# Retention attention and a snake MLP on one core: keys and values of three batches taken in runs of 64 tokens, half of the in-chunk scores left out

## The chip, the cores and the metric

The kernel runs on one core of one Trainium2 chip. The metric is the device time of one execution, in microseconds. The time before is 309.64 us, the median of three runs that lie between 309.6 and 310.09 us.

## The reference

Eight batches of 576 tokens pass through a retention layer with eight heads of 64 elements, and the result, as 4608 rows of 512, through a two-layer MLP with a snake activation:

```
scores = scale * q @ k.T                      # per batch and head
Dmat   = gamma_h ** (i - j) where i >= j, else 0
attn   = (scores * Dmat) @ v
x      = attn, heads side by side             # 4608 x 512
h      = x @ w_in                             # 512 -> 2048
g      = h + sin(alpha * h)**2 / (alpha + 1e-9)
out    = g @ w_out                            # 2048 -> 512
```

Because `Dmat` is zero above the diagonal, a key meets only queries that are not earlier than itself.

## The kernel before

The decay `gamma ** (i - j)` is split into a factor on the keys and one on the queries, both applied when the float32 input is cast to float16 (`cast`, with the factors in the constant tile `cn`). The tokens of a batch are taken as two parts of 256 (`p` = 0, 1) and a tail of 64 (`p` = 2). A part holds two chunks of 128 tokens. Inside a chunk the layer is computed directly: scores, mask, values. What earlier chunks contribute arrives through a 64x64 state for each head and chunk (`outer`, `more`, `to_state`, `add_states`).

**Layout.** `load` brings a part into a tile of 128 partitions by 8 heads by 2 x 64 floats. Partitions 0 to 63 hold the first chunk and 64 to 127 the second. Partition `i` of a chunk holds tokens `2i` and `2i + 1`, which lie next to each other in memory, so a packet of the transfer carries 512 bytes. The index `r` (0 or 1) names the token of the pair. `crossed` turns the cast q and k by DMA transposes into `qT` and `kT`. The tails of two batches share one tile (`raws`, one tile for a pair of batches, each for q, k and v); they come in packets of 256 bytes.

**In-chunk attention.** `scores` is made of matmuls of 64x64 weights. For each head group (`y`, `z`), each half `r` of the keys, each chunk `g` and each half `t` of the heads there is one with 128 query columns: 16 for one call, 64 for a batch. `masked` multiplies a bank pair by a mask of 256 columns (both `r`, 128 queries each) on VectorE and writes float16. `values` multiplies the masked scores by v, again with 64x64 weights and 128 query columns, 64 matmuls for a batch. It comes in two rounds: first those whose rows differ from the bank's half (`same` false), then the others. Between them stands a mark on GpSimd (`told`): a no-op in GpSimd's queue waits for the first round, and the first matmul of the second round waits for that no-op.

**MLP.** Tokens go through the MLP in blocks of 512: the eight batches without their tails, and then the eight tails together. For a block `project(n, u)` makes 128 hidden units (four matmuls of 512 columns), `sine` and `square` run on ScalarE (some squares on VectorE or GpSimd), `product` on VectorE, and `gemm2` makes the output 128 rows at a time. `finish` copies a 128-row result to `osb` and stores it in two transfers.

**Order.** All engines take their instructions in the order in which the program writes them. Up to block 2 that order is written by hand, line by line. From block 3 on a loop writes it: the loop's pass `n` has 16 units `u`; unit `u` issues `project(n, u)`, `sine(n, u)`, what `at_unit(u, ...)` has put there, the square, the product, a quarter of `gemm2(n - 1, ...)`, and then what `behind(u, ...)` has put there. Pass `n` also carries the attention of batch `n + 1` (scores in units 3 and 8, values and state products in unit 12) and, for batch `n + 2`, the casts on GpSimd (units 3 to 8, in the order k0 v0 k1 v1 q0 q1, where the digit is `p`), the states (unit 12) and the transposes (units 13 and 15). The first three loads of batch `n + 3` stand behind units 13 to 15, the other three in units 0 to 2 of the next pass; for batch 5 all six stand in units 0 to 5 of pass 3. The tails of batches `2j` and `2j + 1` are loaded in units 7 to 9 of pass `j + 3`, cast by GpSimd in units 12 to 14 and transposed in unit 15.

All of these loads, transposes and stores are issued by SyncE's queue (SP), one after the other. Each of them waits, besides its data, for the transfer issued eight places earlier on this queue.

```
for i, (nm, p) in enumerate(("k0", "v0", "k1", "v1", "q0", "q1")):
    if n == 3:
        at_unit(i, lambda nm=nm, p=p: load(5, nm, int(p)))
    elif n < 6 and i > 2:
        at_unit(i - 3, lambda nm=nm, p=p: load(n + 2, nm, int(p)))
    if n < 5 and i < 3:
        behind(13 + i, lambda nm=nm, p=p: load(n + 3, nm, int(p)))
    if n < 6:
        at_unit(3 + i, lambda nm=nm, p=p: cast(n + 2, nm, int(p), G_))
```

Of the kernel before, what the change touches and what calls it, by code (L numbers as in the profile page):

```python
# [17 lines left out]
def kernel(  # L18
# [11 lines left out]

    nc = tc.nc

    B, H, S, D = q.shape
# [4 lines left out]
    FC = FF // P  # L40
    KT = DM // P
    NBLK = NT // 512

    gamma = 1.0 - 2.0 ** (-5.0 - np.arange(H, dtype=np.float64))
    scale = 1.0 / np.sqrt(D)
    hi, ii = np.divmod(np.arange(P), 64)
    cn_np = np.zeros((P, 52), dtype=np.float64)
    for h in range(H):
        for r in range(2):
            cn_np[:, 2 * h + r] = gamma[h] ** (64 - (2 * ii + r))  # L50
            cn_np[:, 16 + 2 * h + r] = scale * gamma[h] ** (2 * ii + r - 64)
        cn_np[:, 32 + h] = gamma[h] ** (64 - ii)
        cn_np[:, 40 + h] = scale * gamma[h] ** (ii - 64)
    for a in range(4):
# [8 lines left out]

    ident = const.tile([P, P], F16, tag="ident", bufs=1)
    mask = const.tile([P, 5 * 64], F16, tag="mask", bufs=1)
    cn = const.tile([P, 52], F32, tag="cn", bufs=1)
    fac = {"k": cn[:, 0:16], "q": cn[:, 16:32]}
# [24 lines left out]
    def halves(n):  # L92
        return slice(64 * n, 64 * n + 64)
# [9 lines left out]
    T = {}  # L103

    def load(b, nm, p):
        if p < 2:
            t_ = work.tile([P, H, 2 * D], F32, tag="raw", bufs=6, name=nm + "32")
            nc.sync.dma_start(  # L108
                t_, src[nm][b, :, 256 * p : 256 * p + 256, :].rearrange("h (i r) d -> i h (r d)", r=2)
            )  # L110
        else:
            if b % 2 == 0:
                raw[b, nm, 2] = work.tile([P, H, D], F32, tag="raws", bufs=3, name=nm + "s32")
            t_ = raw[b - b % 2, nm, 2]
            nc.sync.dma_start(t_[halves(b % 2)], src[nm][b, :, 512:576, :].rearrange("h i d -> i h d"))
        raw[b, nm, p] = t_
# [3 lines left out]
    def cast(b, nm, p, eng, ys=(0, 1)):  # L120
# [15 lines left out]
        if p == 2:  # L136
            if nm == "v":
                copy(eng, dst.rearrange("p h d -> p (h d)"), t_.rearrange("p h d -> p (h d)"))
            else:
                eng.tensor_tensor(  # L140
                    dst.rearrange("p a t d -> p t a d"),
                    t_.rearrange("p (t a) d -> p t a d", t=2),
                    fac_s[nm].rearrange("p (t a) -> p t a", t=2).unsqueeze(3).to_broadcast([P, 2, 4, D]),
                    MULT,
                )
        elif nm == "v":
            h0, h1 = 4 * ys[0], 4 * ys[-1] + 4
            copy(
                eng,
                dst[:, h0:h1].rearrange("p h r d -> p (h r d)"),  # L150
                t_[:, h0:h1].rearrange("p h x -> p (h x)"),
            )
        else:
            a0, a1 = 2 * ys[0], 2 * ys[-1] + 2
            n = 2 * (a1 - a0)
            eng.tensor_tensor(  # L156
                dst[:, a0:a1].rearrange("p a r t d -> p t (a r) d"),
                t_.rearrange("p (t a) x -> p t a x", t=2)[:, :, a0:a1].rearrange("p t a (r d) -> p t (a r) d", r=2),
                fac[nm]
                .rearrange("p (t x) -> p t x", t=2)[:, :, 2 * a0 : 2 * a1]  # L160
                .unsqueeze(3)
                .to_broadcast([P, 2, n, D]),
                MULT,
            )
# [63 lines left out]
    class Attention:  # L228
        def __init__(self, b):
            self.b = b  # L230
            self.both = {}
# [87 lines left out]
        def scores(self, p, y, tag):  # L319
            kT, qT = T[self.b, "k", p], T[self.b, "q", p]  # L320
            sc = psum.tile([P, 2, 512], F32, tag=tag, bufs=1, name="sc")
            for z in range(2):
                a = 2 * y + z
                for r in range(2):
                    for g in range(2):
                        for t in range(2):
                            c = 256 * z + 128 * r
                            matmul(  # L328
                                sc[halves(g), t, c : c + 128],
                                kT[halves(t), 2 * a + r, halves(g)],  # L330
                                qT[halves(t), 2 * a : 2 * a + 2, halves(g)],
                                start=(z == 0 and r == 0), stop=True, skip_group_check=True,
                            )
            self.sc[p, y] = sc

        def masked(self, p, y):
            sc = self.sc.pop((p, y))
            ret = work.tile([P, 2, 512], F16, tag="ret", bufs=4, name="ret")
            nc.vector.tensor_tensor(  # L339
                ret.rearrange("p t (z x) -> p (t z) x", z=2),  # L340
                sc.rearrange("p t (z x) -> p (t z) x", z=2),
                mask[:, 0:256].unsqueeze(1).to_broadcast([P, 4, 256]),
                MULT,
            )
            self.ret[p, y] = ret

        def values(self, p, same, *tags, relay=None):
# [12 lines left out]
            made = []  # L360
            for x in range(2):
                for r in range(2):
                    for e in range(2):
                        for g in range(2):
                            t = g if same else 1 - g
                            c = 256 * x + 128 * g
                            m = 256 * e + 128 * r
                            made.append(matmul(  # L368
                                o[t][halves(e), c : c + 128],
                                v16[halves(g), 4 * t + 2 * x + e, r, :],  # L370
                                self.ret[p, x][halves(g), t, m : m + 128],
                                start=(not same and x == 0 and r == 0), stop=False, skip_group_check=True,
                            ))
            if not same and relay is not None:
# [201 lines left out]
    def make_constants():  # L576
# [8 lines left out]
        for g in range(2):  # L585
# [6 lines left out]
            nc.gpsimd.affine_select(  # L592
                out=m, in_=m, compare_op=ge, fill=0.0, base=0, pattern=[[1, 64]], channel_multiplier=-1,
            )

    with tc.manual_schedule():
        nc.scalar.dma_start(cn, cn_dram.ap())
# [479 lines left out]
        at[4].to_state(3, G_)  # L1077
        at[4].to_state(2, G_)
        crossed(4, 0, "q")

        h, m = cycle(("h2", "h0", "h1")), cycle(("m0", "m1"))
        ON_A = (4, 5, 6, 8, 9)
        for n in range(3, NBLK):
# [54 lines left out]
            for u in range(16):  # L1138
# [63 lines left out]
```

## Time and profile before

| | |
|---|---|
| median of the runs | 309.64 us |
| the profiled execution's own time | 310.26 us |
| its span, first to last instruction | 308.5 us |
| granted TensorE clock, mean | 0.989 |
| TensorE busy | 295.6 us, 96% |
| VectorE busy | 206.7 us, 67% |
| ScalarE busy | 181.0 us, 59% |
| GpSimd busy | 135.2 us, 44% |
| moved by DMA | 49.83 MB in 102676 packets |
| packets under 512 bytes | 44640 |

The busy time is the time in which at least one instruction of the engine was under way. In the views of instructions in order of time, a row gives start and length in microseconds, engine, line of the kernel, operation, output and inputs, shape and count; a bracket at its end gives the idle time of the engine before it and what ended that. `PE` is TensorE, `DVE` VectorE, `ACT` ScalarE, `POOL` GpSimd, `SPq` the issuing of transfers on SyncE. Pass 3 of the loop fills about 109 to 140 us of the span, pass 4 140 to 171, pass 5 171 to 202 and pass 6 202 to 233. In what follows a pass is called block 3, 4, 5 or 6.

### The profile page before, as it was taken

What the parts mean: (1) busy time and instruction counts of PE and PEld (TensorE: products, weight loads), DVE (VectorE), ACT (ScalarE), POOL (GpSimd) and SP (SyncE); (2) the same over time, 40 slices, a digit from 0 to 9 for tenths busy, and PEclk for the clock granted to TensorE, in tenths of its full rate; (3) what the DMA queues carried; (4) which work ended last, traced back from release to release, by engine and by line L of the source; (5) the groups of instructions that cost most, each with busy time, mean ns of one, the idle gap of its engine ahead of it and who ended that gap; (6) DMA issues with size and microseconds to landing.
All of it is one profiled execution on the core that took longest, in us unless ns stands there. A gap on an engine that the chain in (4) does not pass through costs nothing.

```text
span 308.5 us, 7866 instructions
## 1 busy us (share of the span) xinstructions
PE 295.6 (96%) x3257; PEld 151.0 (49%) x3257; DVE 206.7 (67%) x298; ACT 181.0 (59%) x286; POOL 135.2 (44%) x150
## 2 busy tenths in 40 slices
PE   6679899999999999999999999999999999999995
PEld 5555456555444544454445444544454454444443
DVE  1686899899669798657765776666666746555600
ACT  1348864675444857674768476857674456555411
POOL 4684772288759589469266926650030000000000
PEclk9599999999999999999999999999999999999999
DMA  7999999999998899879898999763431111111232
GB/s 206 292 228 216 225 249 266 218 262 276 204 213 233 125 231 260 171 111 218 219 261 123 235 213 259 116 130 75 102 70 36 34 36 36 35 34 37 46 89 69
DMA packets 102676, 49.83 MB, mean 162 GB/s; under 512 B 44640, under 2 KB 98160, under 8 KB 102640
## 3 DMA queue, kind: packets, MB, share of 16 engines
q1 hardware_dynamic: 98048, 44.97, 67.0%
q0 software_dynamic: 4224, 4.19, 8.0%
q8 instruction: 25, 0.41, 0.6%
q10 hardware_dynamic: 368, 0.17, 0.2%
q14 instruction: 11, 0.09, 0.1%
HBM read 36.74 MB, written 9.44 MB: 150 GB/s over the span
## 4 chain that ended last, share of the span: by engine, by line
PE 75%; DMA 12%; POOL 5%; issue 3%; ACT 2%; SPq 1%; DVE 0%; POOLq 0%; DVEq 0%; ACTq 0%
PE ops L546 36%; PE hps L503 32%; DMA v<-in_v_dram 5%; DMA q<-in_q_dram 4%; DMA qT<-q 3%; PE o L368 2%; PE sc L328 2%; POOL k L156 1%; POOL q L156 1%; PE kv L269 1%; SPq L108 1%; ACT s_t L511 1%; POOL kvs L311 1%; POOL s L303 1%; PE o L390 1%
## 5 line engine op out<-in xcount | busy, mean ns | idle before, releaser
L546 PE MATMUL ops<-w_out,gT 128*128 128x512 f16 (+2 forms) x592 | 142.5, 374 | 0.3 <-ACT kvs L97 0.2
L527 DVE SCALAR_TENSOR_TENSOR gT<-ss_t,inva,hps 128x512 f16<-128x512 f16 x144 | 106.3, 746 | 52.8 <-ACT ss_t L520 46.0
L511 ACT ACTIVATE s_t<-hps,alpha_t 128x512 f16<-128x512 f32 x144 | 97.4, 687 | 70.7 <-PE hps L503 69.1
L503 PE MATMUL hps<-xT,w_in 128*128 128x512 f16 (+1 forms) x544 | 126.6, 367 | 0.4 <-DMA w_in<-in_moe_w_in_dram 0.2
L503 PEld LDWEIGHTS <-w_in 128*128 128x128 f16 x608 | 58.6, 98 | 64.6 <-DMA w_in<-in_moe_w_in_dram 0.7
L546 PEld LDWEIGHTS <-gT 128*128 128x128 f16 x592 | 56.2, 98 | 64.5 <-issue 0.8
L522 DVE TENSOR_TENSOR ss_t<-s_t 128x512 f16<-128x512 f16 x72 | 40.5, 564 | 17.9 <-ACT s_t L511 17.5
L339 DVE TENSOR_TENSOR ret<-sc,mask 128x1024 f16<-128x1024 f32 x32 | 38.4, 1219 | 3.1 <-PE sc L328 3.1
L520 ACT ACTIVATE ss_t<-s_t 128x512 f16<-128x512 f16 x62 | 38.8, 631 | 0.9
L156 POOL TENSOR_TENSOR q<-q,cn 128x1024 f16<-128x1024 f32 (+1 forms) x16 | 27.4, 1722 | 13.7 <-DMA q<-in_q_dram 13.6
L97 ACT COPY osb<-ops 128x512 f32<-128x512 f32 (+1 forms) x34 | 19.7, 582 | 21.9 <-PE ops L546 20.3
L156 POOL TENSOR_TENSOR k<-k,cn 128x1024 f16<-128x1024 f32 (+1 forms) x13 | 21.7, 1671 | 20.8 <-DMA k<-in_k_dram 16.1
L140 POOL TENSOR_TENSOR ks<-ks,cn 128x512 f16<-128x512 f32 x4 | 4.2, 1044 | 34.2 <-PE o L368 34.2
L311 POOL TENSOR_TENSOR kvs<-s,kvs 128x256 f32<-128x256 f32 x22 | 16.4, 747 | 2.6 <-ACT kvs L97 0.9
L97 ACT CAST xT<-o 128x1024 f16<-128x1024 f32 (+1 forms) x14 | 13.2, 957 | 6.1 <-PE o L390 6.1
L503 PE MATMUL hps<-xS,w_in 128*128 128x512 f16 x64 | 16.4, 379 | 0.0
L522 POOL TENSOR_TENSOR ss_t<-s_t 128x512 f16<-128x512 f16 x10 | 10.8, 1086 | 11.4 <-ACT s_t L511 11.4
L310 POOL TENSOR_TENSOR s<-kvs,cn 128x256 f32<-128x256 f32 x22 | 13.6, 620 | 0.6 <-ACT kvs L97 0.4
L99 POOL CAST v<-v 128x1024 f16<-128x1024 f32 (+1 forms) x10 | 10.2, 1030 | 8.3 <-DMA v<-in_v_dram 8.3
L303 POOL TENSOR_TENSOR s<-kvs,cn 128x256 f16<-128x256 f32 x19 | 12.7, 674 | 1.1 <-issue 0.4
L368 PE MATMUL o<-ret,v 64*64 64x128 f16 x512 | 11.5, 219 | 0.8 <-DVE ret L339 0.4
L328 PE MATMUL sc<-qT,kT 64*64 64x128 f16 x512 | 11.5, 225 | 0.6 <-DMA qT<-q 0.4
(58 smaller groups left out, 139.2 us busy)
## 6 DMA issues: line engine op xcount, KB each, us to landing
out_dram<-osb SPq DMA_DIRECT2D x70, 128.0 KB, 2.5
k<-in_k_dram SPq DMA_DIRECT2D x16, 512.0 KB, 6.8
q<-in_q_dram SPq DMA_DIRECT2D x16, 512.0 KB, 6.9
v<-in_v_dram SPq DMA_DIRECT2D x16, 512.0 KB, 6.3
w_in<-in_moe_w_in_dram POOLq DMA_DIRECT2D x4, 512.0 KB, 12.5
w_out<-in_moe_w_out_dram POOLq DMA_DIRECT2D x4, 512.0 KB, 11.4
ks<-in_k_dram SPq DMA_DIRECT2D x8, 128.0 KB, 4.5
qs<-in_q_dram SPq DMA_DIRECT2D x8, 128.0 KB, 3.6
```

Source lines behind the costliest of these rows:

```text
L97: eng.copy(d_, s_)
L156: eng.tensor_tensor(dst[:, a0:a1].rearrange("p a r t d -> p t (a r) d"), t_.rearrange("p (t a) x -> p t a x", t=2)[:, :, a0:a1].rearrange( ...
L311: nc.gpsimd.tensor_tensor(self.kvs[:, c], s32, self.kvs[:, c], ADD)
L328: matmul(sc[halves(g), t, c : c + 128], kT[halves(t), 2 * a + r, halves(g)], qT[halves(t), 2 * a : 2 * a + 2, halves(g)], start=(z == 0 an ...
L339: nc.vector.tensor_tensor(ret.rearrange("p t (z x) -> p (t z) x", z=2), sc.rearrange("p t (z x) -> p (t z) x", z=2), mask[:, 0:256].unsque ...
L368: made.append(matmul(o[t][halves(e), c : c + 128], v16[halves(g), 4 * t + 2 * x + e, r, :], self.ret[p, x][halves(g), t, m : m + 128], sta ...
L503: matmul(hps_of[n, fc][0][:, cols], w_in16[:, a, fc * P : (fc + 1) * P], xs[n][:, a, cols], start=(a == 0 and part != 1), stop=(a == KT - ...
L511: nc.scalar.activation(s_t, hps, mybir.ActivationFunctionType.Sin, bias=0.0, scale=alpha_t[:, fc : fc + 1],)
L520: nc.scalar.activation(ss_t, s_t, mybir.ActivationFunctionType.Square)
L522: eng.tensor_tensor(ss_t, s_t, s_t, MULT)
L527: nc.vector.scalar_tensor_tensor(gT[n][:, fc, :], ss_t, inva[:, fc : fc + 1], hps, MULT, ADD)
L546: matmul(ops[n, c, cols.start][:, cols], gT[n][:, fk, c * P : (c + 1) * P], w_out16[:, fk, cols], start=(fk == 0), stop=(fk == FC - 1), sk ...
```

## The change

For batches 5, 6 and 7 (`HALVED = 5`) k and v of a part are laid out otherwise: partition `i` of a chunk holds tokens `i` and `64 + i` of it, so `r` = 0 is the first half of the chunk's keys and `r` = 1 the second. The queries keep their layout. A key of the second half meets only queries of the second half, and those are the columns `i >= 32` of both query halves. So the matmuls for `r` = 1 in `scores` and `values` take 64 columns (two runs of 32) where they took 128, and the mask multiply 192 where it took 256, with a mask of its own (`mask_halved`, made on GpSimd in unit 1 of block 3). The decay factors of the keys get 16 further columns in `cn`.

A load of k or v in this layout is made of four transfers of 64 partitions with packets of 256 bytes, where it was one of 128 partitions with packets of 512 bytes.

Three things are moved. The first three loads of batch 5 stand before the loop, the other three in units 0 to 2 of block 3. The tails of `j` = 1 go from block 4 to block 5, and those of `j` = 2 from block 5 to units 0 to 8 of block 6; `j` = 0 and `j` = 3 stay. In blocks 4 to 6 the square of unit 6 goes from ScalarE to VectorE, and that of unit 10 from VectorE to ScalarE.

```diff
+    HALVED = 5
-    cn_np = np.zeros((P, 52), dtype=np.float64)
+    cn_np = np.zeros((P, 68), dtype=np.float64)
+            cn_np[:, 52 + 2 * h + r] = gamma[h] ** (64 - (64 * r + ii))
...
     def load(b, nm, p):
-        if p < 2:
+        if p < 2 and b >= HALVED and nm != "q":
+            t_ = work.tile([P, H, 2 * D], F32, tag="raw", bufs=6, name=nm + "32")
+            for g in range(2):
+                for r in range(2):
+                    s0 = 256 * p + 128 * g + 64 * r
+                    nc.sync.dma_start(
+                        t_[halves(g), :, r * D : r * D + D], src[nm][b, :, s0 : s0 + 64, :].rearrange("h i d -> i h d")
+                    )
+        elif p < 2:
...
# scores
                 for r in range(2):
+                    i0, n = (32, 64) if self.halved and r else (0, 128)
...
-                                sc[halves(g), t, c : c + 128],
+                                sc[halves(g), t, c : c + n],
-                                qT[halves(t), 2 * a : 2 * a + 2, halves(g)],
+                                qT[halves(t), 2 * a : 2 * a + 2, 64 * g + i0 : 64 * g + 64],
...
# masked
+            n, seen = (192, mask_halved) if self.halved else (256, mask[:, 0:256])
-                mask[:, 0:256].unsqueeze(1).to_broadcast([P, 4, 256]),
+                seen.unsqueeze(1).to_broadcast([P, 4, n]),
...
# values
-                                o[t][halves(e), c : c + 128],
+                                o[t][halves(e), c : c + 128].rearrange("p (r i) -> p r i", r=2)[:, :, i0:64],
-                                self.ret[p, x][halves(g), t, m : m + 128],
+                                self.ret[p, x][halves(g), t, m : m + n],
...
+    def make_mask_halved():
+
+        nc.gpsimd.memset(mask_halved, 1.0)
+        for g in range(2):
+            for c0, n in ((0, 64), (128, 32)):
+                m = mask_halved[halves(g), c0 : c0 + 2 * n].rearrange("p (r i) -> p r i", r=2)
+                nc.gpsimd.affine_select(
+                    out=m, in_=m, compare_op=mybir.AluOpType.is_ge, fill=0.0,
+                    base=0, pattern=[[1, 2], [2, n]], channel_multiplier=-1,
+                )
...
# before the loop, and in it
         crossed(4, 0, "q")
+        load(5, "k", 0)
+        load(5, "v", 0)
+        load(5, "k", 1)
...
-                if n == 3:
-                    at_unit(i, lambda nm=nm, p=p: load(5, nm, int(p)))
-                elif n < 6 and i > 2:
+                if n < 6 and i > 2:
...
-            for j in range(n - 3, min(n - 2, 4)):
+            for j, u0 in {3: ((0, 7),), 5: ((1, 7),), 6: ((2, 0), (3, 7))}.get(n, ()):
                 for i, nm in enumerate("kqv"):
-                    at_unit(7 + i, lambda j=j, nm=nm: load(2 * j, nm, 2), lambda j=j, nm=nm: load(2 * j + 1, nm, 2))
-                    at_unit(12 + i, lambda j=j, nm=nm: cast(2 * j, nm, 2, G_))
-                at_unit(15, lambda j=j: crossed(2 * j, 2))
+                    at_unit(u0 + i, lambda j=j, nm=nm: load(2 * j, nm, 2), lambda j=j, nm=nm: load(2 * j + 1, nm, 2))
+                    at_unit(u0 + 5 + i, lambda j=j, nm=nm: cast(2 * j, nm, 2, G_))
+                at_unit(u0 + 8, lambda j=j: crossed(2 * j, 2))
+            if n == 3:
+                at_unit(1, make_mask_halved)
...
-                    square(n, u, A_ if A and u in ON_A else V)
+                    square(n, u, A_ if A and u in (ON_A if n < 4 else (4, 5, 8, 9, 10)) else V)
```

More of the change, by code (lines that the diff above doesn't have):

```diff
@@ L65 @@
     mask = const.tile([P, 5 * 64], F16, tag="mask", bufs=1)
-    cn = const.tile([P, 52], F32, tag="cn", bufs=1)
-    fac = {"k": cn[:, 0:16], "q": cn[:, 16:32]}
+    mask_halved = const.tile([P, 3 * 64], F16, tag="mask_halved", bufs=1)
+    cn = const.tile([P, 68], F32, tag="cn", bufs=1)
+    fac = {"k": cn[:, 0:16], "q": cn[:, 16:32], "halved k": cn[:, 52:68]}
     fac_s = {"k": cn[:, 32:40], "q": cn[:, 40:48]}
@@ L158, in cast @@
                 t_.rearrange("p (t a) x -> p t a x", t=2)[:, :, a0:a1].rearrange("p t a (r d) -> p t (a r) d", r=2),
-                fac[nm]
+                fac["halved k" if nm == "k" and b >= HALVED else nm]
                 .rearrange("p (t x) -> p t x", t=2)[:, :, 2 * a0 : 2 * a1]
@@ L230, in __init__ @@
             self.b = b
+            self.halved = b >= HALVED
             self.both = {}
@@ L338, in masked @@
             ret = work.tile([P, 2, 512], F16, tag="ret", bufs=4, name="ret")
+            n, seen = (192, mask_halved) if self.halved else (256, mask[:, 0:256])
             nc.vector.tensor_tensor(
-                ret.rearrange("p t (z x) -> p (t z) x", z=2),
-                sc.rearrange("p t (z x) -> p (t z) x", z=2),
-                mask[:, 0:256].unsqueeze(1).to_broadcast([P, 4, 256]),
+                ret.rearrange("p t (z x) -> p (t z) x", z=2)[:, :, 0:n],
+                sc.rearrange("p t (z x) -> p (t z) x", z=2)[:, :, 0:n],
+                seen.unsqueeze(1).to_broadcast([P, 4, n]),
                 MULT,
@@ L362, in values @@
                 for r in range(2):
+                    i0, n = (32, 64) if self.halved and r else (0, 128)
                     for e in range(2):
```

## The prediction

> **What bounds the kernel.** I read the page's head first, then the busy time by stage, with borders at unit 12 of each block.
>
> ```profile
> PE 295.6 (96%) x3257; PEld 151.0 (49%) x3257; DVE 206.7 (67%) x298; ACT 181.0 (59%) x286; POOL 135.2 (44%) x150
> ```
> ```profile
> 104.00:134.20 30.20, 30.20 (x348) 14.72 (x340) 24.38 (x34) 20.81 (x33) 19.62 (x19) 1.00 0.90 196
> 134.20:165.25 31.05, 31.05 (x351) 15.13 (x344) 21.23 (x28) 20.96 (x34) 18.98 (x19) 1.00 0.97 204
> 165.25:196.30 31.05, 31.05 (x351) 15.09 (x344) 21.27 (x28) 20.97 (x34) 19.00 (x20) 1.00 0.94 204
> 196.30:227.70 31.40, 31.40 (x291) 14.92 (x285) 20.37 (x29) 21.50 (x34) 9.65 (x15) 1.00 0.54 104
> ```
>
> The columns are the stretch, its length, busy PE, PEld, DVE, ACT and POOL (with counts), granted clock, DMA share and GB/s. From 104 us on PE is busy all the time at full clock; DVE and ACT are busy two thirds of it, POOL less. So a TensorE microsecond saved here is a microsecond of the kernel, and one lost by waiting is lost. DMA is nearly always occupied in the second and third stretch: that is where a dearer transfer can hurt. The change touches nothing of weight before 104 us (the constant tile grows from 52 to 68 columns).
>
> **The narrower matmuls.** PE in unit 12 of block 4, and the tails' scores, in order of time:
>
> ```profile
> 162.34 1.03 PE L503 MATMUL hps<-xT,w_in 128*128 128x512 f16 x4
> 163.29 0.64 PE L368 MATMUL o<-ret,v 64*64 64x128 f16 x32
> 163.76 0.72 PE L269 MATMUL kv<-v,k 64*64 64x64 f16 x64
> 164.30 0.41 PE L368 MATMUL o<-ret,v 64*64 64x128 f16 x16
> ...
> 235.57 0.71 PE L425 MATMUL scs<-qTs,kTs 64*64 64x64 f16 x64
> 236.22 1.04 PE L546 MATMUL ops<-w_out,gT 128*128 128x512 f16 x4
> ```
>
> Lengths overlap, so I take start to start. 32 matmuls of 128 columns take 163.76 - 163.29 = 0.47 us, 14.7 ns each; 64 of 64 columns take 164.30 - 163.76 = 0.54 us, 8.4 ns each. A narrowed one saves 6.3 ns. Half of the 64 score and 64 value matmuls of a batch are narrowed: 64 per batch, 192 in all, 1.2 us, all on the path (0.2 us each for scores and values of a batch). Bounds: 0 if wide and narrow ones in turns all run at the wide pace, or if reading and writing two runs of 32 columns costs what it saves; 1.4 us if half the time goes (7.3 ns). I take 1.2, because the 64-column row is the same 64x64 form, and the tails' scores (64 in 0.65 us with the return to wide matmuls) agree with it.
>
> **The mask and the squares.** Neither is on the path.
>
> ```profile
> L339 DVE TENSOR_TENSOR ret<-sc,mask 128x1024 f16<-128x1024 f32 x32 | 38.4, 1219 | 3.1 <-PE sc L328 3.1
> L520 ACT ACTIVATE ss_t<-s_t 128x512 f16<-128x512 f16 x62 | 38.8, 631 | 0.9
> L587 POOL TENSOR_SCALAR_AFFINE_SELECT mask<-mask 64x256 f16<-64x256 f16 x2 | 0.8, 420 | 0.1
> 161.67 0.69 ACT L511 ACTIVATE s_t<-hps,alpha_t 128x512 f16<-128x512 f32 x1 [1.04 <-PE hps L503]
> ```
>
> A mask multiply falls from 1024 to 768 columns, at most from 1.22 to 0.91 us, twelve times: some 3 us of DVE that nobody waits for. The square of 0.63 us that comes to ACT in unit 10 fits into the 1.04 us that ACT is idle before the next sine; the one that leaves ACT in unit 6 goes to a DVE with 10 us idle in each block. If that cover were gone, a square would cost its 0.63 us in three blocks. The new mask is five small POOL operations, each at most 0.42 us, so at most 2.1 us before the first cast of block 3. The last two casts there waited for their loads (rows below), and POOL has 4.5 us before PE needs its mark.
>
> **The loads.** This is where it can go wrong. SP in order of time: two rows of block 3, the border of blocks 3 and 4, two pairs of tails later.
>
> ```profile
> 109.88 0.57 SPq L108 DMA_DIRECT2D k<-in_k_dram  x1
> ...
> 118.79 1.77 SPq L108 DMA_DIRECT2D q<-in_q_dram  x2
> ...
> 137.10 0.57 SPq L108 DMA_DIRECT2D k<-in_k_dram  x1
> 137.73 0.80 SPq L108 DMA_DIRECT2D v<-in_v_dram  x1
> 138.57 3.63 SPq L179 DMA_TRANSPOSE kT<-k  x1
> 142.32 1.49 SPq L179 DMA_TRANSPOSE qT<-q  x1
> 143.91 1.21 SPq L179 DMA_TRANSPOSE kTs<-ks  x1
> 145.21 1.38 SPq L179 DMA_TRANSPOSE qTs<-qs  x1
> 146.68 1.18 SPq L539 DMA_DIRECT2D out_dram<-osb  x2
> 147.91 0.59 SPq L108 DMA_DIRECT2D k<-in_k_dram  x1
> 148.55 0.67 SPq L108 DMA_DIRECT2D v<-in_v_dram  x1
> 149.27 3.11 SPq L108 DMA_DIRECT2D q<-in_q_dram  x2
> ...
> 154.85 1.38 SPq L115 DMA_DIRECT2D ks<-in_k_dram  x2
> 157.59 1.83 SPq L115 DMA_DIRECT2D qs<-in_q_dram  x2
> ```
>
> The new transfers have the tails' shape: 1.38 us for two, 0.7 us each with the gap. A load of k or v costs SP 2.8 us in place of 0.6, twelve times. On the DMA engines, a stretch of loads of 512-byte packets and one of the tails' 256-byte packets:
>
> ```profile
> 150.50:156.50 6.00, 1.00 1.16 302
> 220.75:221.00 0.25, 1.00 1.16 263
> q1 hardware_dynamic: 3589, 1.81, 115.6%
> q1 hardware_dynamic: 2112, 0.52, 67.1%
> ```
>
> The first two rows are windows (clock, DMA share, GB/s); the others are the queue's packets, MB and time of 16 engines in 150.5 to 156.5 and 220.3 to 223.8. That is 1.156 x 16 x 6.0 / 3589 = 31 ns for a packet of 512 bytes and 0.671 x 16 x 3.5 / 2112 = 18 ns for one of 256. At 302 GB/s a whole load (524 KB) takes 1.75 us of data; four quarters at 18 ns x 32 packets an engine take 0.6 us each, 2.3 to 2.4 us, less than SP's 2.8. So SP's issuing sets the pace.
>
> Who needs these loads, and when? POOL casts k0 v0 k1 v1 q0 q1 in order, and behind them stands the mark for which PE's second round of values waits in unit 12:
>
> ```profile
> 126.76 1.90 POOL L156 TENSOR_TENSOR q<-q,cn 128x1024 f16<-128x1024 f32 x1 [0.32 <-DMA q<-in_q_dram]
> 133.14 1.04 POOL L140 TENSOR_TENSOR ks<-ks,cn 128x512 f16<-128x512 f32 x1 [4.48 <-PE o L368]
> 156.27 3.76 POOL L156 TENSOR_TENSOR q<-q,cn 128x1024 f16<-128x1024 f32 x2 [0.72 <-DMA q<-in_q_dram]
> 164.22 1.04 POOL L140 TENSOR_TENSOR ks<-ks,cn 128x512 f16<-128x512 f32 x1 [4.19 <-PE o L368]
> 186.87 3.76 POOL L156 TENSOR_TENSOR q<-q,cn 128x1024 f16<-128x1024 f32 x2 [0.72 <-DMA q<-in_q_dram]
> 195.28 1.04 POOL L140 TENSOR_TENSOR ks<-ks,cn 128x512 f16<-128x512 f32 x1 [4.64 <-PE o L368]
> ```
>
> The last cast of q ends 4.2 to 4.6 us before PE's first round is done. That idle time is the cover of the loads.
>
> Block 3: the six loads of batch 5 stand together, 16 quarters from 109.9 us (the same place in SP's order) to 121.1, then both q by 122.3. Before, the q loads stood behind a store of unit 3, from 118.8 to 120.6. They are issued some 2 us later; even if they land as much later, 2 us of the 4.5 below stay. The store of unit 3 goes out 5 us later; there are four `osb`.
>
> Block 4 (batch 6), from the rows: eight quarters at 0.7 us from 137.1 to 142.7. The transpose behind them took 3.63 us because data was still queued; now the queue is nearly empty and it takes some 1.3, to 144.0. qT, kTs and qTs end at 148.2, the store at 149.4: 1.6 us later than before. k1 and v1 take eight quarters to 155.1, q0 and q1 are issued by 156.4. A tail's transfer lands 3.6 us after its issue (page 6, median):
>
> ```profile
> vs<-in_v_dram SPq DMA_DIRECT2D x8, 128.0 KB, 3.6
> ```
>
> So the last quarter, issued at 154.4, lands at 158.0, and the q loads follow at 1.75 us of data each, 159.8 and 161.5. q1's cast takes 1.9 us, to 163.4. PE's first round is done at about 164.1 (ks waits for it until 164.22), less the 0.2 us that the scores saved: 163.9. Cover left: 0.5 us of 4.2. I take no wait.
>
> Block 5 (batch 7): SP spends 16 x 0.7 us on quarters in place of 4 x 0.6, 8.8 us more. By block 4's rows it is spared kTs and qTs (2.6 us), which go a block later, the transpose's wait (3.63 less 1.3) and the wait within the pair of q (3.11 less 1.2): 6.8 us. q1 is issued 2.0 us later, with less data queued ahead of it than before; of 4.6 us of cover at least 2.6 stay. In block 6 the DMA share was 0.54 and no k, q or v is loaded; the moved tails have room, and they are needed only in block 7. If the cover of block 4 is used up, the second round of values is late next, and with it all of PE.
>
> Sum: 310.26 us for the profiled execution less 1.2 us is 309.06. That execution lies 0.62 us over the median of the runs; on the median of 309.64 the sum is 308.4 us.
>
> [...]
>
> **Rivals.** (1) Slower: SP issues quarters more slowly when the engines are full. The pair of qs at 157.59 took 1.83 us, 0.92 each; at 0.92 in place of 0.7, sixteen quarters put q1 of batch 6 another 3.5 us back, 3.0 beyond the cover, and PE waits for POOL's mark in unit 12 of block 4: 308.4 + 3.0 = 311.4 us. PE waits from 0.03 us more per quarter on; slower by 0.2% it is from a wait of 1.8 us, 0.14 us per quarter. For it: the busy share of 0.97. Against: the ks pair ran at 0.7 in the same stretch.
>
> (2) Slower packets: a packet of 256 bytes takes the 31 ns of one of 512. A quarter is then 1.0 us of data, which sets the pace: the first eight cost 1.1 us more beyond what the transpose waits anyway, the second eight 0.3 us each, 2.4. q1 lands 3.5 us later than in my sum, a wait of 3.0 us, 311.4 us as well; from a price of 27 ns on it is slower. [...] Against it: 263 GB/s in a window of tails alone, where that price allows half of 302.
>
> (3) No gain: narrowed matmuls between wide ones keep the wide pace: 309.6 us. For it: both kinds share the array in turns, which no row shows. Against: the rows of 64 columns follow rows of 128 at 8.4 ns.
>
> **Chances.** Forecast 0.64, (1) 0.16, (2) 0.05, (3) 0.09, something else 0.06. About 0.2%, 0.6 us, is what a measurement of this kernel can tell from no change. A short wait in block 4 takes part of the gain and leaves "faster" down to 0.6 us. Of (1), 0.01 is a wait that short, 0.03 ends within 0.2% and 0.12 slower; what is left over falls equally on all three. Faster 0.64 + 0.01 + 0.02 = 0.67, within 0.2% 0.09 + 0.03 + 0.02 = 0.14, slower 0.12 + 0.05 + 0.02 = 0.19. The forecast's own range is 308.0 to 309.0 (gain of 0.7 to 1.4 us and 0.2 of spread); with the cases above, which leave 0.1 over its top, 308.0 to 310.8.
>
> **What would show it.** Right: in the stretches of unit 12 the second batch of matmuls in `values` starts with no idle time, scores in units 3 and 8 of blocks 4 to 6 take 0.1 us less each, PE stays fully busy, and quarters of a load stand 0.7 us apart on SP. Wrong: PE idle in unit 12 of block 4 with POOL's q cast ending after 164 us, quarters at 0.9 us and more, or values and scores that take as long as before.

## The result and the profile after

The changed kernel takes 307.15 us, the median of four runs (306.41 to 307.35), against 309.64 before: a ratio of 0.9912, with an interval of 0.9893 to 0.9931. The profiled execution took 307.04 us with a span of 305.3. The forecast was 308.4: the sign was right, but the gain is 2.5 us where 1.2 was forecast, and the time lies below the range.

One thing must be known to read the numbers below: in 34 of 81 executions of the kernels whose load tiles are aligned (a word explained below; the two slowest kernels apart), and in 10 of 106 of the others, TensorE's mean granted clock lay under 0.986 and the time was 0.4 to 6 us longer, so each comparison below is between executions at 0.986 or more, with their count. The kernel before, measured anew beside each set of experiments, has a median of 309.6 to 309.7 us there.

The first view to set against the prediction's is the busy time by stage, of the kernel after. The borders are at the same instructions as in the rows before; the columns are the same.

```profile
101.76:131.98 30.22, 30.22 (x348) 14.75 (x341) 24.39 (x34) 20.80 (x33) 20.84 (x24) 1.00 0.86 194
131.98:162.78 30.80, 30.80 (x350) 14.89 (x345) 20.62 (x29) 20.94 (x34) 17.86 (x18) 1.00 0.80 181
162.78:193.47 30.69, 30.69 (x350) 14.78 (x345) 19.46 (x27) 20.96 (x34) 17.11 (x17) 1.00 0.94 188
193.47:224.52 31.05, 31.05 (x290) 14.64 (x285) 19.33 (x28) 21.52 (x34) 12.30 (x18) 1.00 0.69 148
```

PE is busy without a gap, as before. The first stretch lasts as long as before (30.20). The next three are 0.25, 0.36 and 0.35 us shorter: 0.96 us in all, in place of 1.2. But the first stretch begins at 101.76 us where it began at 104.00. So 2.24 us of the lead were there before any matmul had been narrowed (1.9 by the times of many executions, since the profiled one of the kernel before lies 0.62 us over its median). The prediction had said that nothing of weight changes before 104 us.

So the beginning comes next. The rows show two windows of the kernel before (granted clock, DMA share, GB/s), its queue q1 in 3 to 12 us (packets, MB, time as a share of 16 engines), and the first matmuls:

```profile
2.00:12.00 10.00, 0.85 1.10 282
12.00:30.00 18.00, 0.90 1.19 236
q1 hardware_dynamic: 5304, 2.68, 115.6%
9.80 0.65 PE L269 MATMUL kv<-v,k 64*64 64x64 f16 x32 [3.28 <-ACT v L97]
37.22 2.76 PE L503 MATMUL hps<-xT,w_in 128*128 128x512 f16 x16
```

The same of the kernel after:

```profile
2.00:12.00 10.00, 0.91 1.10 323
12.00:30.00 18.00, 0.86 1.19 236
q1 hardware_dynamic: 6123, 3.09, 113.9%
8.96 0.45 PE L283 MATMUL kv<-v,k 64*64 64x64 f16 x32 [1.86 <-ACT v L102]
35.23 2.76 PE L520 MATMUL hps<-xT,w_in 128*128 128x512 f16 x16
```

The same loads, in the same order and by the same code, run at 323 GB/s where they ran at 282. A packet of 512 bytes takes 1.139 x 16 x 9.0 us / 6123 = 26.8 ns of an engine, and it took 1.156 x 16 x 9.0 / 5304 = 31.4. PE, which waits for the first casts, starts 0.84 us earlier, and is 1.99 us ahead at the row of 37.22 us. The granted clock does not explain it: it is higher in one window and lower in the next.

What had changed for these loads is where their tiles lie in SBUF. Tiles are placed one behind the other. `cn` has grown by 16 floats (64 bytes a partition) and `mask_halved` takes 384 bytes, so every tile allocated after them moves by 448 bytes. The addresses that the two builds assigned (bytes from the start of a partition, as a multiple of 256 and a rest):

```
                          before                         after
load tiles (k32 ...)      60480 = 236 x 256 +  64        60928 = 238 x 256
w_in16                    18336 =  71 x 256 + 160        18784 =  73 x 256 + 96
```

The load tiles are 4096 bytes each, so all six buffers start alike. Before, each packet of 512 bytes began 64 bytes beyond a multiple of 256; after, it begins at one. "Aligned" below means that the load tiles begin at a multiple of 256.

### The profile page after: what moved, and what is told of

It is laid out like the page before. It is cut to its first block, busy times and chain, and to the rows that moved or that the text cites. A ratio compares the mean times of both kernels' runs of the same rounds, so it can differ in the third digit from the quotient of the medians.

```text
span 305.3 us, 7926 instructions
## 1 busy us (share of the span) xinstructions
PE 294.7 (97%) x3257; PEld 150.2 (49%) x3257; DVE 203.6 (67%) x298; ACT 181.0 (59%) x286; POOL 136.7 (45%) x155
## 4 chain that ended last, share of the span: by engine, by line
PE 87%; DVE 5%; POOL 2%; DMA 2%; ACT 1%; issue 1%; SPq 1%; DVEq 0%; ACTq 0%; POOLq 0%
PE ops L563 40%; PE hps L520 39%; PE sc L343 2%; PE o L385 2%; DMA q<-in_q_dram 2%; DVE ret L355 2%; PE kv L283 1%; DVE k L169 1%; DVE gT L544 1%; SPq L121 1%; PE o L407 1%; ACT s_t L528 1%; POOL k L169 1%; POOL q L169 1%; DVE xT L104 1%
## 5 line engine op out<-in xcount | busy, mean ns | idle before, releaser
L539 DVE TENSOR_TENSOR ss_t<-s_t 128x512 f16<-128x512 f16 x72 | 39.5, 549 | 18.9 <-ACT s_t L528 18.2
L169 POOL TENSOR_TENSOR k<-k,cn 128x1024 f16<-128x1024 f32 (+1 forms) x13 | 21.9, 1685 | 22.8 <-DMA k<-in_k_dram 17.6
L355 DVE TENSOR_TENSOR ret<-sc,mask 128x1024 f16<-128x1024 f32 x20 | 23.8, 1219 | 2.2 <-PE sc L343 2.2
L385 PE MATMUL o<-ret,v 64*64 64x128 f16 (+1 forms) x512 | 11.1, 215 | 0.9 <-DVE ret L355 0.4
L355 DVE TENSOR_TENSOR ret<-sc,mask_halved 128x768 f16<-128x768 f32 x12 | 11.4, 951 | 0.0
```

The costliest lines, as they stand in the source:

```text
L169: eng.tensor_tensor(dst[:, a0:a1].rearrange("p a r t d -> p t (a r) d"), t_.rearrange("p (t a) x -> p t a x", t=2)[:, :, a0:a1].rearrange( ...
L355: nc.vector.tensor_tensor(ret.rearrange("p t (z x) -> p (t z) x", z=2)[:, :, 0:n], sc.rearrange("p t (z x) -> p (t z) x", z=2)[:, :, 0:n], ...
L385: made.append(matmul(o[t][halves(e), c : c + 128].rearrange("p (r i) -> p r i", r=2)[:, :, i0:64], v16[halves(g), 4 * t + 2 * x + e, r, :] ...
L539: eng.tensor_tensor(ss_t, s_t, s_t, MULT)
```

## The experiments

Theory A: the aligned load tiles give the early gain of about 1.9 us, and the narrower matmuls some 0.7 to 0.9. Its rival: the gain is one of the halved layout or of the moved steps, and the addresses are chance. A second question is whether the quarter loads are as free as the prediction had them.

### Only the addresses, on the kernel before

```diff
     xS = const.tile([P, KT, 512], F16, tag="xS", bufs=1)
+    const.tile([P, 96], F16, tag="pad", bufs=1, name="pad")
```

> The kernel before with an unused constant tile of 192 bytes per partition, so that every tile after the constants, the six load tiles first, starts at a multiple of 256 bytes (it was 64 beyond one, as in the kernel before). Nothing else changes. Theory A (the gain that my sum lacks comes from where the load tiles start): the first whole loads run at about 345 GB/s in place of 290, and the time is 309.64 less 1.5, near 308.1 us. Theory B (the early gain has another cause: the longer constant table, the program's new length, chance): no change, 309.6 us.

An unused tile of 192 bytes moves the load tiles of the kernel before to 60672, a multiple of 256. It took 307.76 us (all five executions, 307.68 to 308.14), ratio 0.9943, interval 0.9931 to 0.9955. Its rows answer to those above:

```profile
2.00:12.00 10.00, 0.92 1.10 326
8.94 0.45 PE L270 MATMUL kv<-v,k 64*64 64x64 f16 x32 [1.81 <-ACT v L98]
35.18 2.76 PE L504 MATMUL hps<-xT,w_in 128*128 128x512 f16 x16
```

A tile that nothing reads or writes gives 1.9 us, with the start of the kernel after to within 0.05 us. Theory A holds for that part of the gain. In twelve traces of this case the order is the same without exception: 320 to 326 GB/s in 2 to 12 us in the nine with aligned load tiles, 279 to 283 in the three without.

### The addresses of the kernel before, in the kernel after

```diff
     xS = const.tile([P, KT, 512], F16, tag="xS", bufs=1)
+    const.tile([P, 32], F16, tag="pad", bufs=1, name="pad")
```

> The changed kernel with an unused tile of 64 bytes, so that the same tiles start 64 bytes beyond a multiple of 256, as in the kernel before. Theory A: the early part is again as slow as before and only the narrower matmuls are left, 309.64 less 0.9, near 308.7 us, with first loads at 290 GB/s. Theory B: as the changed kernel, 307.15 us.

With 64 unused bytes the load tiles of the changed kernel lie 64 bytes beyond a multiple of 256 again. Ten of twelve executions: 308.89 us median (308.51 to 310.55).

```profile
2.00:12.00 10.00, 0.87 1.09 279
9.85 0.64 PE L284 MATMUL kv<-v,k 64*64 64x64 f16 x32 [3.11 <-ACT v L103]
```

The early gain is gone: without the alignment the changed kernel is 1.6 us slower (308.89 against 307.26). Against before 0.75 us are left: what the change does where it was meant to. This is 0.45 less than the 1.2 that I had forecast for it.

### Which tiles, and which offsets

First, the load tiles alone: 64 bytes more behind them put all later work tiles (casts, transposed tiles, `osb`) back to where they lay modulo 256.

```diff
+    const.tile([P, 96], F16, tag="pad", bufs=1, name="pad")
...
         load(0, "k", 0)
+        work.tile([P, 32], F16, tag="pad2", bufs=1, name="pad2")
```

> The kernel before with 192 bytes ahead of the six load tiles and 64 behind them: only the load tiles of q, k and v start at a multiple of 256 bytes, and everything that is cast, transposed or stored starts 64 bytes beyond one, as in the kernel before. Theory A, by the loads: as with 192 bytes alone, near 308.1 us. Theory A2, by the transposes or stores: 309.6 us. Between, if both share.

```profile
2.00:12.00 10.00, 0.86 1.08 320
```

Five of twelve executions: 307.73 us (307.10 to 308.36). That is the time with all of them moved: the load tiles make the difference, not the tiles that transposes and stores use.

Then an offset of 128, on the kernel before:

```diff
+    const.tile([P, 32], F16, tag="pad", bufs=1, name="pad")
```

> The kernel before with an unused constant tile of 64 bytes: the load tiles begin 128 bytes beyond a multiple of 256 (before: 64 beyond). Theory that only the multiple of 256 counts (a packet of 512 bytes then touches 3 aligned pieces of 256 in place of 2): as before, 309.6 us, 280 to 290 GB/s in 2 to 12 us. Theory that 128 is enough (or that 64 beyond is the bad case by itself): as with 192 bytes, 307.8 us and 320 GB/s.

```profile
2.00:12.00 10.00, 0.90 1.13 283
q1 hardware_dynamic: 5313, 2.68, 118.2%
```

Ten of twelve: 310.0 us (309.62 to 310.42), the speed of the kernel before. Half of 256 is no better than a quarter of it: 1.182 x 16 x 9.0 / 5313 = 32.0 ns for a packet of 512 bytes, against 31.4 at 64 and 26.8 at 0.

Last, the weights, which both kernels load to addresses that are no multiple of 256; here they and all that lies behind them are aligned, in the changed kernel.

```diff
+    const.tile([P, 80], F16, tag="pad1", bufs=1, name="pad1")
     w_in16 = const.tile([P, KT, FF], F16, tag="w_in16", bufs=1)
...
     xS = const.tile([P, KT, 512], F16, tag="xS", bufs=1)
+    const.tile([P, 48], F16, tag="pad", bufs=1, name="pad")
```

> The changed kernel with 160 unused bytes ahead of the weights' tiles and 96 behind them: w_in16 and w_out16 then begin at a multiple of 256 bytes too (before: 96 beyond one), and the load tiles still do. Theory: what counts is where a transfer's packets begin in SBUF; the weights' loads write packets of 1024 bytes and more, of which a smaller share is cut off by a wrong beginning, so they gain less, but they run in the first 30 us, where every load is waited for: 0 to 0.8 us below the changed kernel, 306.4 to 307.15. Rival: only 512-byte packets suffer: 307.15.

Nine of twelve: 306.88 us (306.35 to 307.61), the lowest of all kernels here, ratio 0.9929 over all twelve. The changed kernel's own nine of sixteen (the first four and those below) have a median of 307.26. The 0.4 us between them come from different sets of runs and their ranges overlap, so that the weights gain anything is open.

### Without the halved layout

```diff
-    HALVED = 5
+    HALVED = 8
```

> The changed kernel with no batch in the new layout: wide matmuls, whole loads and wide masks everywhere, while the moved tails and loads, the swapped squares, the new mask's making and the places of the tiles stay. Theory A: the narrower matmuls are worth 0.9 us and the rest of the gain stays, near 308.1 us. Theory B2 (the moves gave the early gain): the same time; it is told apart by the run with 192 bytes. If the quartered loads had cost anything, this would be nearer to the changed kernel's 307.15.

Here the tiles are aligned and the steps are moved, but no batch is halved. Five of twelve: 307.78 us (307.6 to 308.29). That is e1's time; so the halved layout gives what lies between this and the changed kernel, 0.5 us by the medians. With the 0.75 from the other side, and 0.96 us in the profiled executions of before and after, it is worth 0.5 to 1.0 us.

The traces narrow this down, because PE never waits in this part. From the first to the last border of the stretches above it takes 123.70 us in the kernel before, 123.73 with 192 unused bytes and 123.75 with quarter loads and wide matmuls (the next experiment). It takes 122.78 and 122.66 in the two traces of the changed kernel, 122.96 with 64 unused bytes and 122.81 with aligned weights. So the narrow matmuls save 0.7 to 1.0 us, whatever the addresses, and in these traces the quarters cost nothing that shows.

### The loads without the narrow matmuls

```diff
-    i0, n = (32, 64) if self.halved and r else (0, 128)
+    i0, n = (0, 128)                                       # in scores and values
-    n, seen = (192, mask_halved) if self.halved else (256, mask[:, 0:256])
+    n, seen = (256, mask_halved) if self.halved else (256, mask[:, 0:256])
+    const.tile([P, 64], F16, tag="pad", bufs=1, name="pad")   # after xS, load tiles aligned
```

> The changed kernel with its quarter loads, moved tails and a mask of its own for the halved keys, but with every score and value matmul at the full 128 columns (the mask has 256 columns in place of 192, and zeros do what the narrow matmuls skipped); the load tiles begin at a multiple of 256 bytes. Theory: the narrow matmuls are all that the halved layout gives, and the quarters cost nothing on the path. Then this kernel stands where the changed kernel without any halved batch stands, 307.8 us (307.6 to 308.2), 0.6 to 0.7 us above the changed kernel. Rival: the quarters cost something that the narrow matmuls pay for (block 4 gave only 0.05 us in unit 12): then it is above 308.2 us, and unit 12 of block 4 shows PE idle.

Eight of twelve: 308.08 us (307.55 to 309.65), five of them from 307.55 to 308.17 and three above 309. The median is where theory has it (307.6 to 308.2); the three above 309 I can't explain. In its trace (an execution of 311.7 us) the matmuls of scores take as long as before again, and unit 12 of block 4 has no wait:

```profile
196.20 0.81 PE L284 MATMUL kv<-v,k 64*64 64x64 f16 x64
196.83 0.41 PE L386 MATMUL o<-ret,v 64*64 64x128 f16 x16
```

These are block 5's rows, the only ones of unit 12 with a gap: from 196.20 to 196.83 are 0.63 us where 0.53 is usual. So the quarters cost PE at most 0.1 us in this execution; the medians (308.08 against 307.78 without quarters) leave room for 0.3. The wider mask also moves the weights by 128 bytes, which no run sets apart.

### What the quarter loads cost if there are more of them

Each quarter is split once more, by heads: eight transfers a load, with the same packets and bytes.

```diff
-                    nc.sync.dma_start(t_[halves(g), :, ...], src[nm][b, :, ...])
+                    for t in range(2):
+                        hs = slice(4 * t, 4 * t + 4)
+                        nc.sync.dma_start(t_[halves(g), hs, ...], src[nm][b, hs, ...])
```

> The changed kernel with eight transfers for each load of k and v of batches 5 to 7 in place of four (each quarter once more split by four heads). It doubles SP's work, the rival's suspected cost, and shows where the cover ends. If an issue has a fixed price (a whole load of 512 KB takes 0.57 us, a quarter 0.68), an eighth takes 0.6 to 0.7 us, a load 5 us and more; in block 4 q1 of batch 6 comes some 10 us later. There the cast of q1 already starts only 1.3 us before PE goes on, so PE waits some 8 to 10 us in unit 12 of block 4, and some more in block 5, where 3.5 us of cover are left: 315 to 325 us. If the price goes by size (0.34 us for an eighth), nothing changes: 307.2 us.

It took 333.39 us (four executions, 332.84 to 334.84), ratio 1.0755, interval 1.0715 to 1.0795: more than I expected. SP, then GpSimd and PE (block 4's unit 12), PE's waits from 104 to 262 us, and two stages:

```profile
145.83 5.34 SPq L118 DMA_DIRECT2D k<-in_k_dram  x8
151.22 5.23 SPq L118 DMA_DIRECT2D v<-in_v_dram  x8
...
179.12 3.76 POOL L172 TENSOR_TENSOR q<-q,cn 128x1024 f16<-128x1024 f32 x2 [1.60 <-DMA q<-in_q_dram]
...
177.57 0.64 PE L286 MATMUL kv<-v,k 64*64 64x64 f16 x32 [6.29 <-POOL v L104]
180.67 0.53 PE L388 MATMUL o<-ret,v 64*64 64x128 f16 x16 [2.45 <-POOLq L240]
...
PE kv L286 <- POOL v L104: 10.4, 3, 6.3
PE o L388 <- POOLq L240: 8.3, 3, 3.4
...
104.00:140.00 36.00, 30.52 (x324) 14.95 (x327) 24.67 (x35) 20.95 (x34) 19.12 (x23) 0.94 0.66 144
140.00:182.00 42.00, 33.26 (x372) 16.23 (x360) 20.34 (x27) 21.55 (x34) 18.87 (x20) 0.87 0.64 149
```

An eighth of 64 KB costs SP 0.65 to 0.67 us, as much as a quarter of 128 KB (0.67 to 0.68): here the price goes by the transfer and not by its size. PE waits in unit 12 of blocks 3, 4 and 5, 18.7 us in all, first for the cast of v and then for GpSimd's mark. The rest of the 26 us, some 7, goes in part with the granted clock: PE is busy 122.3 us with the 480 matmuls of `hps` from `xT` with 512 columns in place of 119.9, and 21.6 with those of `o` in place of 19.5, and the clock, in place of 1.00, is 0.94 and 0.87 in the two stages shown. So the rival of dear quarters was the right fear: at 0.68 us a quarter they are covered, and at twice that the kernel loses 26 us.

### The moved tails

```diff
-            for j, u0 in {3: ((0, 7),), 5: ((1, 7),), 6: ((2, 0), (3, 7))}.get(n, ()):
+            for j, u0 in {3: ((0, 7),), 4: ((1, 7),), 5: ((2, 7),), 6: ((3, 7),)}.get(n, ()):
```

> The changed kernel with the second and third pair of tails' transfers, casts and transposes back in blocks 4 and 5, at the units they had before. SP issues 6 more transfers and waits for two more transposes' input in block 4 and 5. By the prediction's step on the loads, in block 5 the move spares SP 2.6 us, so without it q1's cast of batch 7 ends 2.6 us later, with at least 2.6 us of cover: no wait, 307.15 us as the changed kernel. In block 4 the tails come behind the loads in SP's order, so nothing of the loads moves. Rival: SP is then late for batch 7 by more than the cover (the waits of transposes for tails' casts stand ahead of the loads), PE idles in unit 12 of block 5: 308 us or more.

Six of twelve: 308.3 us (307.29 to 309.38), against 307.26: by the medians the move is worth about 1 us, though the ranges overlap. The only trace is of an execution of 314.56 us; its granted clock is 1.00 from 184 to 196 us, and its block 5 shows a wait that the changed kernel hasn't:

```profile
184.76 2.72 SPq L116 DMA_DIRECT2D k<-in_k_dram  x4
...
198.76 1.90 POOL L169 TENSOR_TENSOR q<-q,cn 128x1024 f16<-128x1024 f32 x1 [1.69 <-DMA q<-in_q_dram]
...
195.04 0.54 PE L385 MATMUL o<-ret,v 64*64 64x128 f16 x32
195.41 0.80 PE L283 MATMUL kv<-v,k 64*64 64x64 f16 x64
198.79 0.53 PE L385 MATMUL o<-ret,v 64*64 64x128 f16 x16 [2.58 <-POOLq L237]
```

I had expected no wait. The loads of k1 stand 195.04 - 184.76 = 10.3 us before PE's unit 12, and in the changed kernel 191.67 - 177.15 = 14.5 (rows below): 4.2 us later and not 2.6. The first loads of batch 7 are 2.4 us late already (172.10 where the changed kernel has 166.29, both set against PE's unit 12): the six transfers of the tails in block 4 hold up SP as well, not only the two transposes. q's second load then lands after PE is ready. How much of this wait the executions of 308.3 us have, no trace shows.

### One batch more

```diff
-    HALVED = 5
+    HALVED = 4
```

> The changed kernel with batch 4 in the halved layout too (HALVED = 4), nothing else moved. Its loads are issued in block 2, between transposes and stores. By the matmuls it gains another 0.3 us (scores 0.2, values 0.1 as in block 4 of the changed kernel): 306.8 us. If block 2 has no cover for 8.4 us more of SP's issuing, PE waits in unit 12 of block 2 or in block 3's scores: above 307.5 us.

It took 314.45 us (six executions, 310.23 to 314.96, ratio 1.0105, all at a mean clock below 0.986). In the trace, of the execution of 310.23 us, the second load of v of batch 4 leaves SP at 97.0 us, behind three other loads in quarters, where the changed kernel has 92.3. ScalarE's cast of it starts at 99.93 in place of 96.39, and PE stands still for it in block 2:

```profile
101.02 0.19 PE L283 MATMUL kv<-v,k 64*64 64x64 f16 x1 [2.17 <-ACT v L102]
```

This wait alone is more than the 0.3 us that the matmuls of one batch give, so no gain is to be had there with the loads as they are placed. Why the other five executions take 3 to 5 us more is not shown.

### The changed kernel again

> The changed kernel once more, beside the other two, since its first time stands on four runs: 307.15 us. By the theory that aligned load tiles give 1.9 us and narrow matmuls 0.6 to 0.7, 306.9 to 307.4; a second group of runs some 3 us above it, with a lower granted clock in the first 30 us, as in the kernels with aligned tiles so far.

Twelve further executions have a ratio of 0.9969 (0.9942 to 0.9997) over all of them; the five at a clock of 0.986 or more took 307.11 to 309.05 us, median 307.6. The median of all sixteen executions is 308.04 us. That the first four all came at 0.986 or more was luck, and by that median the gain is 1.6 us and not 2.5. The same holds for the aligned kernels of the experiments: over all twelve executions of each, e3, e4, e5 and e7 have ratios of 0.9987 to 0.9999.

The traces show where the gain is lost. In those of e4, e5 and e7 (312.34, 311.7 and 314.56 us) the first loads run at 325 or 326 GB/s all the same. But from 12 to 30 us the granted clock is 0.73, 0.65 and 0.65, where it is 0.86 to 0.89 in the traces of e1, e3, e8 and the changed kernel's two. In that of e5 PE's scores wait 1.9 us for VectorE's mask multiplies between 17 and 21 us; in that of e3 they wait 1.0 us, and in those of e1 and of the first profile of the changed kernel not at all. Why that wait comes in some executions and not in others, and whether the clock is lower because of it, stays open.

## Why the prediction was right and wrong

**"The change touches nothing of weight before 104 us (the constant tile grows from 52 to 68 columns)": wrong, and this is the step that failed.** I had the cause in my hand, a constant tile that grows, and costed it as 16 floats. What it does is move all later tiles; it aligned the load tiles, which is worth 1.9 us by the kernel before with 192 unused bytes, and nothing of it is left in the kernel after with 64 more. That the new sizes added up to a multiple of 256 was chance. A packet of 512 bytes took 26.8 ns of an engine in the aligned tiles, 31.4 (17% more) at 64 bytes beyond a multiple of 256 and 32.0 (19% more) at 128. What a packet spends this time on, no run shows.

**The narrower matmuls: the mechanism right, the size 0.7 to 1.0 for 1.2 us (0.96 in the profiled execution).** The rows after, block 5 as an example:

```profile
174.97 0.54 PE L343 MATMUL sc<-qT,kT 64*64 64x128 f16 x32
191.67 0.54 PE L385 MATMUL o<-ret,v 64*64 64x128 f16 x32
192.04 0.72 PE L283 MATMUL kv<-v,k 64*64 64x64 f16 x64
192.57 0.36 PE L385 MATMUL o<-ret,v 64*64 64x128 f16 x16
192.75 0.38 PE L407 MATMUL o<-qT,s 64*64 64x128 f16 x8
192.90 0.41 PE L385 MATMUL o<-ret,v 64*64 64x128 f16 x16
193.13 0.41 PE L407 MATMUL o<-qT,s 64*64 64x128 f16 x16
```

The first round of values takes 192.04 - 191.67 = 0.37 us where it took 0.47: 16 narrowed ones save 0.10 us, 6.3 ns each, to the digit. Scores save the same 0.1 in each of six calls, 0.58 us in all. What is short is in unit 12: it saves 0.05, 0.16 and 0.14 us in blocks 4, 5 and 6 in place of 0.2. In block 4 the matmuls of `kv` before the second round, 64 as always, take 161.83 - 161.23 = 0.60 us in place of 0.53 (rows below), and the last sixteen matmuls of values start 0.20 us after the states' before them, in place of 0.12. The profile names no releaser for these gaps, and I leave them open. The second trace of the changed kernel has the gap of block 4 again (0.59 us) but not that of block 5, which saves 0.25 us there. The rival of no gain fell: the 32 matmuls of a round, half of them narrow and in turns with wide ones, take 0.37 us where 0.47 was the wide pace.

**The mask and the squares: right.** The multiply takes 0.95 us, where I had put 0.91 as the lowest it could fall to; from 104 us to the end PE waits for nothing in this execution, so not for it either:

```profile
L355 DVE TENSOR_TENSOR ret<-sc,mask_halved 128x768 f16<-128x768 f32 x12 | 11.4, 951 | 0.0
```

**The loads: the price right, the cover more than computed.** SP in blocks 4 and 5, then GpSimd and PE in block 4, after:

```profile
147.48 2.72 SPq L116 DMA_DIRECT2D k<-in_k_dram  x4
150.25 2.67 SPq L116 DMA_DIRECT2D v<-in_v_dram  x4
152.96 2.46 SPq L121 DMA_DIRECT2D q<-in_q_dram  x2
...
177.15 2.71 SPq L116 DMA_DIRECT2D k<-in_k_dram  x4
...
158.41 1.90 POOL L169 TENSOR_TENSOR q<-q,cn 128x1024 f16<-128x1024 f32 x1
160.49 1.91 POOL L169 TENSOR_TENSOR q<-q,cn 128x1024 f16<-128x1024 f32 x1 [0.18 <-DMA q<-in_q_dram]
...
160.86 0.54 PE L385 MATMUL o<-ret,v 64*64 64x128 f16 x32
161.23 0.79 PE L283 MATMUL kv<-v,k 64*64 64x64 f16 x64
161.83 0.36 PE L385 MATMUL o<-ret,v 64*64 64x128 f16 x16
162.01 0.30 PE L407 MATMUL o<-qT,s 64*64 64x128 f16 x8
162.21 0.41 PE L385 MATMUL o<-ret,v 64*64 64x128 f16 x16
```

A quarter costs SP 0.68 us, as forecast (0.7). q1's cast ends at 162.40 us; PE is ready for its second round at about 161.76. By the prediction's reckoning, in which the mark waits for the cast's end, PE would have waited 0.6 us here. It went on at 161.83. The rows of the unmoved tails above say why: there the second round starts at 198.79, with the cast that began at 198.76 still to run 1.9 us. In the rows of the eighths it starts at 180.67, and the second of the two casts begins only at about 181.0 (two casts of 1.90 us from 179.12 on). So in these rows the mark did not wait for the cast ahead of it to end; that it passes once that cast's load has landed would agree with them. In block 4 that load was there at 160.49 at the latest, when the cast began, and 161.8 - 160.5 = 1.3 us were left. That no wait came, as forecast, was luck, since two errors met: by the cast's end the forecast had 0.5 us left and there were 0.6 too few, 1.1 us worse than computed, and the mark passes 1.9 us earlier than I had it.

**Rivals (1) and (2)** did not come: quarters at 0.68, and PE without a wait for them. The bound of 27 ns in rival (2) was off by its own terms: 0.5 us of cover and a wait of 1.8 us make 2.3 us, with the 1.3 us that the transpose waits anyway 3.6 us over 16 quarters, so 0.92 us for the 32 packets that a quarter gives each engine, some 29 ns a packet. Its price did not come: in the changed kernel, from 166.5 to 171.5 us, 3399 packets of the quarters took 74.7% of 16 engines' time, 0.747 x 16 x 5.0 / 3399 = 17.6 ns each. By the prediction's 18 and 31 ns, two packets of 256 bytes took 16% longer than one of 512 in tiles that begin 64 beyond a multiple of 256; in the aligned tiles it is 2 x 17.6 against 26.8, 31%. The mechanism of both, SP's time ending in PE's wait for the mark, is the one that the eighths set off.

## What to carry to other kernels

Before calling a change of a constant tile free, work out the addresses of everything that is allocated behind it: in this kernel 192 unused bytes are worth 1.9 us in the executions at the higher clock, more than the whole of the computation that the change leaves out. Count enough executions before believing such a gain, since 34 of 81 executions of the aligned kernels, at a lower granted clock, took 0.4 to 6 us longer. Look first at the tiles that are loaded while the engines wait for them, in this kernel in packets of 512 bytes, and try letting them begin at a multiple of 256 bytes, as here. Where a load was cut into more transfers here, its queue paid for their number, 0.65 to 0.68 us each for 64 and for 128 KB; so count what the queue has left before the first engine waits.

## What the runs showed of the hardware that I had not expected

- From 3 to 12 us, packets of 512 bytes that begin at a multiple of 256 in SBUF took 26.8 ns of an engine (the changed kernel); those that begin 64 or 128 beyond one took 31.4 (the kernel before) and 32.0 (the kernel before with 64 unused bytes).
- A transfer of 64 KB took 0.65 to 0.67 us of SP's time (the eighths, from 145.83 us), one of 128 KB 0.67 to 0.68 (the changed kernel, from 147.48), one of 512 KB 0.57 (the kernel before, at 137.10).
- A no-op in GpSimd's queue did not wait for the end of the cast ahead of it in two traces: PE, which waits for it, went on 0.03 us after the start of a cast of 1.9 us with the tails unmoved, and 0.3 us before the start of one with the eighths.
- TensorE's granted clock was lower around waits of PE. With the eighths it is 0.87 from 140 to 182 us, where PE waits 6.29 and 2.45 us, and four matmuls of `hps` take 1.78 us behind these waits where they took 1.03 ahead of them. With the tails unmoved it is 0.92 from 196 to 199 us, where PE waits 2.58 us, and 1.00 in the three windows of 3 us before. In the changed kernel it is 1.00 in all four stretches from 101.76 to 224.52 us, where PE waits for nothing. That the waits lower the clock, no run sets apart.
